# A fused adaLN / sliding-attention / token-MLP block on one core: modulation blocks on ScalarE's queue, x in two loads, other warming matmuls, another order

## The chip, the cores and the metric

The kernel runs on one core of one Trainium2 chip. A core has TensorE (PE in the profile; PEld are its weight loads), VectorE (DVE), ScalarE (ACT), GpSimd (POOL) and SyncE (SP), which issues DMAs. The metric is the device time of one execution in microseconds; 203.5 us is the median of three runs before the change (203.14 to 203.56).

## The reference

x is 2048 tokens by 512 channels. A conditioning vector c gives six modulation vectors; two of them act in the first layernorm, one scales the attention's output, two act in the second layernorm, and one scales the MLP's output. Attention has 32 heads of 16 channels, and each token looks at itself and at 7 earlier tokens, two apart. The MLP mixes over tokens (2048 to 1792 to 2048), not over channels.

```python
mod = (_silu(c) @ w_mod).reshape(c.shape[0], 6, 1, -1)      # sa, ca, ga, sb, cb, gb
h = _layernorm(x) * (1 + ca) + sa
x = x + ga * _A_ref(h, A_wqkv, A_wo)                        # local attention: W = 8, dilation 2
h = _layernorm(x) * (1 + cb) + sb
x = x + gb * _B_ref(h, B_w1, B_b1, B_w2, B_b2)              # layernorm, gelu(h.T @ w1 + b1) @ w2 + b2, transposed back
```

## The kernel before

The program is a list of named operations with their dependencies (`_Graph`). The text `ORDER` lists every name in the order of issue; `name:a` or `name:v` puts an operation that can run on two engines on ScalarE or VectorE, and a digit gives it one of four PSUM slots `ps0` to `ps3` of two banks each. `schedule()` checks that the order respects the dependencies, and each engine executes its own operations in that order. A DMA is an instruction of the queue that issues it: `dma(...)` takes SP's unless it is told `"act"`. So an engine whose next instruction waits holds back all that stand behind it, DMAs too. All operations are recorded through one helper, so nearly all profile rows have the line L179, and one goes by tiles.

The start. `ld_c` loads c, and `cps` (TensorE) turns it into a column, `silu_exp` (ScalarE) and `silu_dve` (VectorE) make silu of it. `ld_wmodA` and `ld_wmodB` bring two halves of the columns of `w_mod` that the first layernorm needs (512 KB each, rows of 2 KB) into the buffer `vD0`. `modcols0` and `modcols1` multiply them by silu(c) into columns, and `modcols_h` and `modcols_cp` bring these to SBUF as `sacol` and `a1col`. Meanwhile tokens 0 to 511 (chunk 0: four tiles of 128 tokens, loaded by `ld_x00`, `ld_x01`, `ld_x02`) get their layernorm: `ln1s` (statistics: two VectorE instructions, or four of ScalarE), `rstd1` (Ln and Exp on ScalarE, with one Ln for each run of neighbouring tiles whose statistics came from the same engine), `nb1`, `ln1n` (the normalised tile). `tr0_..` transposes them on TensorE, and `hT0_0` to `hT0_3` evict them to `hTb`, with scale `a1col` and shift `sacol`. `warm0` to `warm4` are matmuls of the identity with itself, whose result nobody reads.

Then four chunks of 512 tokens run, interleaved. For each: projections `qkvk`, `qkvq`, `qkvv` (TensorE) with evictions `evk`, `evq`, `evv`; `vd` copies that spread v over partitions by window position (16 DMAs a chunk on SP); `qk0` to `qk3` (VectorE products q times shifted k) with `red` (TensorE sums them per head); `max`, `sub`, `exp`, `sum`, `rb`, `smul` (the softmax); `a2` and its eviction `a2ev`; `pv0` to `pv3` (VectorE, weights times v) with `pvacc`; `oev`; `wo` (output projection plus residual); `x1ev`, `x1sq`, `rstd2`, `t`, `aff` (second layernorm), `ln3s`, `rstd3`, `h3` (the MLP's own layernorm). The MLP's first matmul is done in two halves over tokens: `mlp1_0_<fc><fl>_0` and `_4` take chunks 0 and 1, `park0` keeps that half in SBUF as bf16, and `mlp1_1_..` take chunks 2 and 3; `gadd`, `gelu` and `gbm` finish it. `mlp2` is the second matmul, `xb` prepares x plus bias, `fin` adds, `st_out` stores. `modrows` makes the other four modulation vectors from `ld_wmod2` to `ld_wmod5`; `biascols` brings the biases in as columns; `ld_w1_..` and `ld_w2_..` load the MLP's weights into buffers that became free.

Of the kernel before, what the change touches and what calls it, by code (L numbers as in the profile page):

```python
# [32 lines left out]
evk0_0:v ln1s8:a qkvq0_1:1 ln1n4:v ln1n5:v ld_wmod2 qkvv0_0:0 evq0_0:v evk0_1:a ln1n7:v evq0_1:a qk0_0 ln1s10:a  # L33
tr1_10:2 tr1_00:3 qkvq0_2:1 evv0_0:a hT1_0:v qk0_1 hT1_2:a qkvv0_2:0 hT1_1:a rstd1_2_0 evq0_2:a nb1_2_0 ln1n11:v
red0_0:3 ln1n9:v hT1_3:a red0_1 qk0_2 biascols:1 evv0_2:a qkvk1_0:2 ln1s12:a vd0_130 vd0_121 qkvq1_0:0 qk0_3 vd0_111
khalo1:a ln1s14:a vd0_030 vd0_010 red0_2 evk1_0:a biascols_cp ld_wo1 red0_3 ln1n8:v ln1n10:v vd0_100 qkvq1_2:1
evq1_0:a max0 vd0_031 ln1s15:a vd0_000 qk1_0 sub0 vd0_020 qkvk1_2:2 vd0_001 exp0 vd0_131 evq1_2:a qk1_1 vd0_011 sum0
vd0_120 tr2_10:0 rb0 red1_0:1 ld_wo3 evk1_2:a modrows:3 vd0_110 smul0 hT2_2:a vd0_021 qk1_2 a2_0:2 vd0_101 hT2_3:a
red1_1 mrow_ev tr2_00:0 a2ev0:a bc0 qkvv1_2:3 qk1_3 ln1s13:a qkvv1_0:2 hT2_0:a pv0_0 hT2_1:a red1_2 khalo2:a rstd1_3_0
red1_3 evv1_0:a qkvq2_0:0 nb1_3_0 max1 vhalo1:a evv1_2:a pv0_1 ln1n15:a pvacc0_0:2 vd1_031 sub1 ln1n12:a vd1_000  # L40
qkvk2_0:3 exp1 vd1_001 vd1_030 pv0_2 ln1n13:a vd1_130 sum1 evq2_0:a vd1_011 pvacc0_1 evk2_0:a vd1_100 qkvv2_2:0 pv0_3
vd1_010 oev0_1:a vd1_020 rb1 vd1_131 qkvk2_2:3 evv2_2:a vd1_021 gmul vd1_110 ln1n14:a pvacc0_2:2 vd1_120 smul1
evk2_2:a pvacc0_3 vd1_101 qk2_0 a2_1:1 oev0_3:a tr3_00:0 vd1_111 tr3_10:3 vd1_121 a2ev1:a wo2:2 bc2 qk2_1 hT3_2:a
ld_w1_0_3 wo3:1 bc1 hT3_3:a hT3_0:a wo1:3 x1ev3 pv1_0 x1ev2 wo0:1 hT3_1:a x1ev1 qkvq2_2:2 pv1_1 x1sq3 x1sq2 pvacc1_0:0
x1ev0 x1sq1 pv1_2 pvacc1_1 qkvv2_0:3 x1sq0 khalo3:a rstd2_0_0 vhalo2:a evq2_2:a nb2_0_0 pv1_3 warm2:1 t2:a red2_0:1
red2_1 evv2_0:a pvacc1_2:2 qk2_2 pvacc1_3 oev1_1:a vd2_010 qkvq3_0:3 vd2_100 oev1_3:a vd2_030 t1:a vd2_000 t3:v wo7:0
qk2_3 evq3_0:a vd2_120 vd2_110 wo6:2 t0:a vd2_111 x1ev7 wo5:3 vd2_021 aff0_0 x1ev6 vd2_020 x1sq7 wo4:0 ld_w1_0_1 x1sq6
vd2_031 red2_2 x1ev5 ld_w1_0_0 ln3s0_0:v red2_3 x1ev4 qkvk3_0:2 ln3s0_2:v ln3s0_3:v vhalo3:a x1sq5 x1sq4 qkvv3_0:3
ln3s0_1:v vd2_121 rstd2_1_0 evk3_0:a vd2_101 nb2_1_0 max2 t4:a qk3_0 sub2 t6:a qkvk3_2:0 rstd3_0_0 t7:a evv3_0:a
nb3_0_0 qkvv3_2:2 t5:v h3_2:v h3_0:v exp2 aff1_0 evk3_2:a sum2 qkvq3_2:3 evv3_2:a h3_1:v rb2 vd3_031 h3_3:v ln3s1_1:a  # L50
smul2 mlp1_0_10_0:0 vd3_020 ln3s1_0:v vd2_131 mlp1_0_30_0:2 ln3s1_3:a vd3_030 ln3s1_2:v mlp1_0_11_0 ld_w1_0_6 qk3_1
vd2_011 a2_2:1 evq3_2:a mlp1_0_31_0 vd2_001 rstd3_1_0 ld_w1_0_4 mlp1_0_00_0:3 a2ev2:a nb3_1_0 h3_5:v mlp1_0_01_0
h3_4:v h3_7:a pv2_0 red3_0:1 h3_6:a red3_1 mlp1_0_31_4 qk3_2 vd3_110 mlp1_0_10_4 vd2_130 mlp1_0_01_4 vd3_001
mlp1_0_11_4 vd3_130 qk3_3 vd3_000 mlp1_0_00_4 park0_1:a red3_2 park0_0:a pvacc2_0:0 pv2_1 red3_3 mlp1_0_60_0:3
mlp1_0_60_4 max3 vd3_121 pvacc2_1 mlp1_0_30_4 vd3_011 oev2_1:a pv2_2 vd3_101 sub3 vd3_010 mlp1_0_40_0:0 exp3 vd3_120
mlp1_0_41_0 park0_3:a vd3_021 pv2_3 sum3 vd3_111 mlp1_0_61_0 rb3 vd3_100 pvacc2_2:2 vd3_131 smul3 pvacc2_3 ld_w1_0_2
ld_w1_0_5 a2_3:1 oev2_3:a mlp1_0_61_4 a2ev3:v wo9:2 park0_6:a pv3_0 wo8:1 x1ev9 ld_w1_1_0 x1sq9 mlp1_0_41_4 pv3_1
x1ev8 wo11:3 ld_w1_1_3 pvacc3_0:2 x1ev11 wo10:1 pv3_2 x1sq11 ld_w1_1_1 x1sq8 pvacc3_1 mlp1_0_40_4 x1ev10 pv3_3 x1sq10
mlp1_0_20_0:3 oev3_1:a mlp1_0_21_0 rstd2_2_0 pvacc3_2:1 nb2_2_0 t11:v pvacc3_3 t10:a t9:v mlp1_0_21_4 t8:v oev3_3:a
aff2_0 mlp1_0_20_4 park0_4:a wo13:2 ld_w1_1_2 park0_2:a ld_w1_1_5 wo12:1 bc3 x1ev13 ln3s2_0:v x1sq13 ln3s2_2:v wo14:0  # L60
ld_w2_0 x1ev12 ln3s2_3:v wo15:3 x1sq12 ln3s2_1:v rstd2_3_0 mlp1_0_50_0:2 rstd3_2_0 nb2_3_0 t13:v mlp1_0_50_4 x1ev15
nb3_2_0 ld_w2_7 h3_9:v x1ev14 h3_8:v mlp1_0_51_0 h3_10:v x1sq15 t12:v h3_11:v mlp1_0_51_4 x1sq14 aff3_0 mlp1_1_00_0:1
rstd2_3_2 park0_5:a nb2_3_2 mlp1_1_30_0:3 t14:v t15:v ln3s3_0:a aff3_2 mlp1_1_31_0 ld_w2_2 mlp1_1_50_0:0 ln3s3_1:a
ln3s3_3:v mlp1_1_51_0 ln3s3_2:v mlp1_1_01_0 rstd3_3_0 rstd3_3_2 mlp1_1_10_0:2 nb3_3_0 h3_13:v ld_w1_1_4 h3_12:a
nb3_3_2 h3_14:v mlp1_1_11_0 h3_15:v xb2 mlp1_1_11_4 ld_w1_1_6 mlp1_1_10_4 mlp1_1_00_4 gadd1 ld_w2_3 mlp1_1_31_4 gelu2
mlp1_1_01_4 gelu3 mlp1_1_30_4 gadd0 mlp1_1_50_4 ld_w2_1 gadd3 gelu1 mlp1_1_51_4 gelu0 mlp1_1_20_0:2 gelu7 mlp1_1_21_0
gelu6 gbm7 gbm0 mlp1_1_21_4 gbm3 ld_w2_6 gadd5 mlp1_1_20_4 gbm1 gelu11 mlp1_1_40_0:1 gadd2 mlp1_1_41_0 gbm6 gelu5
mlp1_1_40_4 gbm2 ld_w2_4 gbm11 gelu10 gbm5 mlp1_1_41_4 gelu4 mlp1_1_60_0:3 gadd4 mlp1_1_61_0 gbm4 gelu8 mlp1_1_60_4
gbm10 gelu9 gbm8 mlp1_1_61_4 gbm9 xb1 mlp2_1_0_0:0 gadd6 xb3 gelu13 gelu12 mlp2_0_0_0:2 gbm12 gbm13 mlp2_5_0_0:1
mlp2_1_12_0 mlp2_3_0_0:3 fin1_0 xb0 st_out1_0 mlp2_3_12_0 mlp2_2_0_0:0 fin3_0 st_out3_0 ld_w2_5 mlp2_2_12_0 xb7  # L70
mlp2_6_0_0:3 fin2_0 xb5 st_out2_0 mlp2_6_12_0 mlp2_4_0_0:0 xb6 fin6_0 mlp2_0_12_0 mlp2_5_12_0 fin0_0 mlp2_8_0_0:3
fin5_0 st_out5_0 st_out6_0 st_out0_0 mlp2_7_0_0:2 xb4 mlp2_4_12_0 mlp2_10_0_0:1 fin4_0 st_out4_0 mlp2_8_12_0 xb8
mlp2_7_12_0 mlp2_11_0_0:0 fin7_0 fin8_0 st_out8_0 st_out7_0 mlp2_13_0_0:2 xb11 xb9 mlp2_11_12_0 xb10 mlp2_10_12_0
mlp2_9_0_0:3 fin10_0 fin11_0 st_out10_0 mlp2_9_12_0 xb14 mlp2_15_0_0:1 fin9_0 st_out9_0 mlp2_15_12_0 mlp2_13_12_0
st_out11_0 mlp2_12_0_0:0 xb15 xb12 mlp2_12_12_0 xb13 mlp2_14_0_0:3 fin13_0 fin12_0 st_out12_0 st_out13_0 mlp2_14_12_0
mlp2_15_0_256:2 fin14_0 fin15_0 st_out14_0 mlp2_15_12_256 st_out15_0 fin15_256 st_out15_256
"""


# [864 lines left out]
```

## Time and profile before

| what | value |
|---|---|
| median of three runs | 203.5 us (203.14 to 203.56) |
| the profiled execution's own time | 205.16 us |
| its span, first to last instruction | 203.5 us |
| mean granted TensorE clock | 0.992 |
| busy in the span | PE 194.1, DVE 157.6, ACT 126.3, POOL 4.3 us |
| eight warming matmuls of `warm0` | 1.42 to 5.01 |
| landing of the second modulation block | 9.86 |
| first ScalarE eviction of a transposed tile (`hT0_2`) | 12.18 |
| first projection matmul | 13.21 |
| end of `a2ev2` (ScalarE, attention weights of chunk 2) | 91.71 |
| end of the last product of chunk 3 (VectorE) | 98.44 |
| last normalised tile of the MLP (`h3_15`) | 134.55 |

Times inside the execution are microseconds from the start of the span. A busy time counts instructions that the engine executes; matmuls overlap one another, and the ends of TensorE's rows are modelled, so its real progress is read from starts: a matmul with 512 columns starts every 0.216 us at full clock and every 0.427 us at half. On VectorE and ScalarE an instruction of some size starts about 0.1 us before the one ahead of it has ended.

### The profile page before, as it was taken

The numbers are of one execution on the slowest core, as the hardware profiler recorded it, in microseconds if no ns is written. First come the engines' busy times: TensorE is split into PE (matmuls) and PEld (weight loads), VectorE is DVE, ScalarE is ACT, GpSimd is POOL, SyncE is SP. The second block draws the span as 40 slices with busy tenths as digits, with TensorE's granted clock in tenths as the row PEclk, the third lists the DMA queues.
The fourth block names the chain that finished last, engine by engine and source line by source line (L and its number), as shares of the span: only waits on it lengthen the run. The fifth ranks groups of instructions, "written<-read, shape, count | busy, mean of one in ns | idle before, by whom it ended". The sixth has DMA issues, their size and how long they took to land.

```text
span 203.5 us, 3374 instructions
## 1 busy us (share of the span) xinstructions
PE 194.1 (95%) x1276; PEld 91.4 (45%) x1296; DVE 157.6 (77%) x206; ACT 126.3 (62%) x261; POOL 4.3 (2%) x30
## 2 busy tenths in 40 slices
...
GB/s 132 332 358 269 297 90 164 161 101 109 177 162 137 93 153 252 33 212 221 68 180 204 293 95 314 290 290 293 290 212 0 29 138 94 77 26 55 71 56 53
DMA packets 42179, 33.48 MB, mean 165 GB/s; under 512 B 2100, under 2 KB 39604, under 8 KB 42164
## 3 DMA queue, kind: packets, MB, share of 16 engines
...
q14 instruction: 5, 0.04, 0.1%
q10 hardware_dynamic: 8, 0.00, 0.0%
...
## 4 chain that ended last, share of the span: by engine, by line
PE 56%; ACT 33%; DMA 3%; issue 3%; DVE 3%; SPq 1%; ACTq 0%; DVEq 0%
PE ps L179 56%; ACT junk L179 8%; ACT hTb L179 4%; DMA vD<-in_w_mod_dram 3%; ACT v_c L179 3%; ACT k_c L179 3%; ACT q_sb L179 3%; ACT h L179 2%; ACT xx L179 2%; ACT o_sb L179 2%; ACT lv L179 2%; DVE prod L179 1%; ACT n_sb L179 1%; DVE pvb L179 1%; ACT ee L179 1%
## 5 line engine op out<-in xcount | busy, mean ns | idle before, releaser
L179 DVE TENSOR_TENSOR prod<-q_sb,k_c 128x4096 bf16<-128x4096 bf16 x16 | 36.1, 2282 | 0.0
L179 DVE TENSOR_TENSOR pvb<-a2sb,vD 128x4096 bf16<-128x4096 bf16 x16 | 35.9, 2285 | 0.1
L179 PE MATMUL ps<-h,wst 128*128 128x512 bf16 x125 | 29.0, 380 | 0.3 <-issue 0.2
L179 PEld LDWEIGHTS <-wst 128*128 128x128 bf16 x128 | 12.2, 98 | 15.8 <-issue 1.6
L179 PE MATMUL ps<-gT,vD 128*128 128x512 bf16 x81 | 18.6, 379 | 0.2
L179 PE MATMUL ps<-woq,o_sb 128*128 128x512 bf16 x62 | 16.3, 379 | 0.1
L179 PE MATMUL ps<-hTb,w_k 128*128 128x512 bf16 x61 | 15.1, 385 | 0.6 <-ACT hTb L179 0.5
L179 DVE TENSOR_TENSOR k_c<-ps,k_c 128x512 bf16<-128x512 f32 (+1 forms) x9 | 5.5, 631 | 12.9 <-PE ps L179 10.8
L179 PE MATMUL ps<-hTb,w_q 128*128 128x512 bf16 x62 | 15.2, 381 | 0.1
L179 DVE TENSOR_TENSOR q_sb<-ps,q_sb 128x512 bf16<-128x512 f32 x8 | 5.4, 689 | 12.6 <-PE ps L179 12.5
L179 PEld LDWEIGHTS <-o_sb 128*128 128x128 bf16 x106 | 10.3, 98 | 10.2 <-issue 0.9
L179 PEld LDWEIGHTS <-w_q 128*128 128x128 bf16 x96 | 9.9, 109 | 10.9 <-issue 1.9
L179 PE MATMUL ps<-hTb,w_v 128*128 128x512 bf16 x62 | 14.7, 380 | 0.1
L179 PEld LDWEIGHTS <-vD 128*128 128x128 bf16 x116 | 9.1, 97 | 12.2 <-DMA vD<-in_w_mod_dram 2.3
L179 PEld LDWEIGHTS <-w_k 128*128 128x128 bf16 x80 | 8.9, 112 | 9.5 <-issue 1.7
L179 PE MATMUL ps<-gT,prod 128*128 128x512 bf16 x56 | 12.6, 379 | 0.0
L179 PE MATMUL ps<-gT,pvb 128*128 128x512 bf16 x55 | 12.5, 379 | 0.1
L179 PEld LDWEIGHTS <-w_v 128*128 128x128 bf16 x80 | 8.5, 111 | 8.6 <-issue 0.8
L179 ACT ACTIVATE junk<-xx,su 128x512 bf16<-128x512 bf16 x16 | 11.6, 725 | 0.4
L179 PEld LDWEIGHTS <-ident 128*128 128x128 bf16 (+1 forms) x79 | 7.1, 107 | 9.6 <-issue 4.5
L179 ACT ACTIVATE hTb<-ps,sacol,a1col 128x512 bf16<-128x512 bf16 x12 | 8.8, 784 | 3.4 <-PE ps L179 3.4
L179 ACT ACTIVATE o_sb<-ps 128x1024 bf16<-128x1024 f32 x8 | 8.0, 1019 | 4.4 <-PE ps L179 4.4
...
## 6 DMA issues: line engine op xcount, KB each, us to landing
...
```

Source lines behind the costliest of these rows:

```text
L179: r = fn(*a, **k)
```

## The change

- `ld_wmodA` and `ld_wmodB` are issued by ScalarE's queue. There the order is `ld_c`, `act_table`, `ld_wmodA`, `silu_exp`, `ld_wmodB`, `rstd1_0_0`.
- Chunk 0's x comes in two loads of two tiles each, `ld_x00` first; `ld_x01` is gone.
- The warming matmuls are nine groups (8, 6, 4, 4, 3, 3, 3, 2, 2) and no longer five (8, 4, 3, 3, 3): `warm0`; then `warm1`, `warm3` and `warm6` before the first transposes; `warm8` and `warm2` between the last transposes of chunk 0 and the first projection; `warm5` among the `wo` of chunk 1; `warm7` and `warm4` among the first `mlp1`.
- The order is new on every engine, and 28 operations change between ScalarE and VectorE, all of them statistics, norms or small evictions (`ln1s`, `ln1n`, `ln3s`, `t`, `h3`, `evk0_0`, `evq0_0`). On GpSimd `halo0` comes before `consts2`.

```diff
-consts ld_x02 ld_c consts2 warm0:0 ld_x01 act_table ld_x00 ld_wmodA ld_wmodB ld_b1 ln1s3:v ln1s2:a ld_b2 cps:1 ln1s0:v
-warm3:2 ld_x1 halo0 ld_w1a silu_exp ln1s1:v rstd1_0_2 ld_w1b warm1:3 ld_x2 nb1_0_2 silu_dve rstd1_0_0 ld_w0 ln1n2:a
-modcols0:0 nb1_0_0 ln1n0:v ld_w2 modcols1 ln1n1:v ln1n3:a sc_rep tr0_10:2 modcols_h tr0_00:3 modcols_cp tr0_02
-ld_wmod5 tr0_12 hT0_0:v warm4:1 hT0_2:a hT0_1:v ln1s7:a hT0_3:v ld_wo2 qkvk0_0:0 ln1s5:v ld_wo0 qkvk0_2:1 ld_wmod4
-ln1s6:v ln1s4:a ln1s9:v ld_wmod3 qkvk0_1:3 rstd1_1_0 ln1s11:v qkvk0_0b evk0_2:a qkvq0_0:2 nb1_1_0 ld_x3 ln1n6:v
...
+consts ld_x00 ld_c halo0 consts2 warm0:0 cps:1 ld_x02 act_table ld_wmodA silu_exp ld_wmodB ld_x1 ld_w1a ld_w1b ld_x2
+ld_w0 ln1s0:v ln1s1:v rstd1_0_0 ln1s3:a silu_dve sc_rep nb1_0_0 ln1s2:v ln1n1:v ln1n0:v rstd1_0_2 ld_w2 ld_x3 ld_wmod4
+ld_wo0 ld_b1 ld_wmod5 ld_b2 ld_wmod3 ld_wmod2 nb1_0_2 ln1n2:v ln1n3:v warm1:2 warm3:3 warm6:0 tr0_10:1 modcols0:2
+modcols1 tr0_00:3 tr0_02 tr0_12 modcols_h modcols_cp hT0_0:v hT0_1:v hT0_2:a hT0_3:v ln1s4:v ln1s5:v warm8:0 warm2:2
+qkvk0_0:0 qkvk0_0b qkvk0_2:3 qkvk0_1:2 ln1s6:a ln1s7:a evk0_2:a rstd1_1_0 evk0_0:a qkvq0_0:1 qkvq0_1:3 qkvv0_2:0
+ln1s9:v ln1s10:v ln1s11:v nb1_1_0 ln1s8:v evq0_0:a ln1n6:a ln1n7:a evk0_1:a evq0_1:a evv0_2:a rstd1_2_0 ln1n5:v
...
+oev1_3:a qkvq3_0:2 wo7:0 qk2_3 t3:v qk2_2 t1:a t2:a khalo3:a evq3_0:a x1ev7 aff0_0 wo6:3 red2_2 red2_3 wo4:2 warm5:0
+wo5:0 x1ev6 vhalo3:a x1sq6 x1sq7 x1ev4 ln3s0_3:a x1ev5 x1sq4 x1sq5 max2 ln3s0_0:v ln3s0_1:v ln3s0_2:v qk3_0 qkvk3_2:3
...
+ld_w1_0_4 vd3_020 vd3_001 ld_w1_0_6 vd2_101 mlp1_0_30_0:0 warm7:1 mlp1_0_10_0:2 a2_2:1 mlp1_0_11_0 warm4:3 mlp1_0_31_0
+red3_0:3 qk3_1 a2ev2:a nb3_1_0 red3_1 h3_6:v h3_5:v h3_4:a h3_7:a mlp1_0_00_0:1 mlp1_0_01_0 pv2_0 qk3_3 qk3_2
+mlp1_0_01_4 mlp1_0_00_4 mlp1_0_10_4 mlp1_0_31_4 mlp1_0_30_4 mlp1_0_11_4 park0_0:a park0_3:a park0_1:a pv2_1 red3_2
+red3_3 mlp1_0_60_0:1 pvacc2_0:0 max3 pvacc2_1 mlp1_0_61_0 sub3 pv2_2 oev2_1:a exp3 pv2_3 mlp1_0_60_4 mlp1_0_61_4 sum3
...
+ln3s2_3:v ln3s2_2:v ln3s2_1:v x1sq13 x1ev12 x1sq12 rstd2_3_0 rstd3_2_0 xb3 nb3_2_0 h3_9:v h3_11:v nb2_3_0 h3_8:v t12:v
...
+mlp2_7_12_0 mlp2_6_12_0 xb5 fin5_0 xb6 fin6_0 xb4 xb7 fin4_0 fin7_0 st_out4_0 st_out7_0 st_out6_0 st_out5_0 ld_w2_6
+ld_w2_7 mlp2_9_0_0:0 mlp2_11_0_0:1 mlp2_11_12_0 mlp2_8_0_0:2 mlp2_8_12_0 mlp2_10_0_0:3 mlp2_10_12_0 mlp2_9_12_0 xb8
...
@@ -240,7 +240,7 @@
-    WARM=(8, 4, 3, 3, 3),
+    WARM=(8, 6, 4, 4, 3, 3, 3, 2, 2),
...
@@ -387,11 +387,11 @@
     dma(c_t[:], c[0].rearrange("(t p) -> t p", p=P), 1024, [], ["c_t"], "ld_c", "act")
-    for i, n_ in ((0, 1), (1, 1), (2, 2)):
+    for i, n_ in ((0, 2), (2, 2)):
         dma(xx[:, i:i + n_, :], x_view[:, i:i + n_, :], n_ * P * D * 2, [], [("xx", i + k) for k in range(n_)],
             f"ld_x0{i}")
-    dma(wmodA[:, 0:2, :], wmod_view[:, 0:2, 0:2 * D], 2 * D * P * 2 * 2, [], vdk[0][4:], "ld_wmodA")
-    dma(wmodA[:, 2:4, :], wmod_view[:, 2:4, 0:2 * D], 2 * D * P * 2 * 2, [], vdk[0][:4], "ld_wmodB")
+    dma(wmodA[:, 0:2, :], wmod_view[:, 0:2, 0:2 * D], 2 * D * P * 2 * 2, [], vdk[0][4:], "ld_wmodA", "act")
+    dma(wmodA[:, 2:4, :], wmod_view[:, 2:4, 0:2 * D], 2 * D * P * 2 * 2, [], vdk[0][:4], "ld_wmodB", "act")
```

More of the change, by code (lines that the diff above doesn't have):

```diff
@@ L33 @@
[L33 to L76, printed above, removed]
+consts ld_x00 ld_c halo0 consts2 warm0:0 cps:1 ld_x02 act_table ld_wmodA silu_exp ld_wmodB ld_x1 ld_w1a ld_w1b ld_x2
@@ new lines @@
+ln1n4:v qk0_0 qk0_1 qkvq0_2:1 tr1_10:2 tr1_00:3 qkvv0_0:0 evq0_2:a hT1_2:a khalo1:a hT1_3:a hT1_0:v nb1_2_0 ln1s12:v
+ln1n11:v hT1_1:a evv0_0:a red0_0:1 red0_1 qkvk1_0:2 biascols:3 qkvq1_0:0 ln1s13:a ln1n10:a ln1n8:a evk1_0:a evq1_0:a
+ln1s14:a vd0_010 vd0_030 vd0_021 ld_wo3 vd0_101 vd0_000 vd0_020 vd0_111 vd0_001 vd0_011 ld_wo2 vd0_121 vd0_110 vd0_100
+vd0_120 vd0_031 qk0_2 qk0_3 biascols_cp ln1n9:v red0_2 red0_3 qkvq1_2:3 max0 sub0 qkvk1_2:2 evq1_2:a exp0 qk1_0 qk1_1
+sum0 tr2_10:0 red1_0:3 evk1_2:a rb0 modrows:2 smul0 hT2_2:a khalo2:a hT2_3:a mrow_ev vhalo1:a qk1_2 red1_1 tr2_00:1
@@ new lines @@
+a2_0:0 qk1_3 hT2_0:a a2ev0:a qkvv1_2:2 qkvv1_0:0 pv0_0 ln1s15:a hT2_1:a evv1_2:a rstd1_3_0 evv1_0:a qkvk2_2:1
+pvacc0_0:2 red1_2 red1_3 nb1_3_0 pv0_1 max1 qkvq2_0:0 pvacc0_1 sub1 ln1n13:a evk2_2:a ln1n12:a ln1n15:a ln1n14:a
+evq2_0:a exp1 qkvk2_0:1 tr3_00:0 sum1 vd0_130 ld_wo1 bc0 vd0_131 vd1_001 vd1_030 vd1_011 vd1_010 vd1_021 vd1_000
+vd1_020 vd1_120 vd1_121 vd1_031 vd1_131 vd1_110 vd1_100 vd1_130 bc1 vd1_111 vd1_101 oev0_1:a evk2_0:a rb1 hT3_0:a
+pv0_2 pv0_3 gmul smul1 qkvv2_2:2 pvacc0_2:1 pvacc0_3 a2_1:3 evv2_2:a oev0_3:a hT3_1:a vhalo2:a a2ev1:a qkvv2_0:2
@@ new lines @@
+mlp1_0_20_0:3 x1ev10 x1sq10 x1sq11 rstd2_2_0 oev3_1:a mlp1_0_21_0 mlp1_0_21_4 pvacc3_2:1 pv3_3 nb2_2_0 t8:a t10:v
+t11:v t9:v pvacc3_3 mlp1_0_20_4 oev3_3:a aff2_0 mlp1_0_40_4 park0_2:a wo13:0 park0_4:a wo12:1 x1ev13 ln3s2_0:v
+ln3s2_3:v ln3s2_2:v ln3s2_1:v x1sq13 x1ev12 x1sq12 rstd2_3_0 rstd3_2_0 xb3 nb3_2_0 h3_9:v h3_11:v nb2_3_0 h3_8:v t12:v
+t13:v h3_10:v wo15:3 wo14:2 mlp1_0_50_0:0 mlp1_0_51_0 mlp1_0_51_4 mlp1_0_50_4 x1ev14 x1ev15 x1sq15 x1sq14 aff3_0
+rstd2_3_2 nb2_3_2 park0_5:a ln3s3_0:a ln3s3_1:a mlp1_1_10_0:1 mlp1_1_11_0 mlp1_1_00_0:2 mlp1_1_01_0 mlp1_1_50_0:3
```

20 lines of the change are left out of this document (added).

## The prediction

> **What bounds the kernel now.** I read the chain that ended last first, whole and then in order of time. Its engine line says that TensorE is busy on only 56% of it and ScalarE carries 33%; columns of the pieces are start, length, what (all us).
>
> ```profile
> PE 56%; ACT 33%; DMA 3%; issue 3%; DVE 3%; SPq 1%; ACTq 0%; DVEq 0%
> ```
>
> ```profile
> 2.74 7.11 DMA vD<-in_w_mod_dram
> 9.86 0.05 issue
> 9.90 2.25 PE ps L179 x32
> 12.16 0.02 issue
> 12.18 0.78 ACT hTb L179
> ...
> 90.59 0.21 ACT rs L179
> 90.81 0.02 issue
> 90.83 0.17 DVE nb L179
> ...
> 96.15 2.29 DVE prod L179
> 98.45 0.04 issue
> 98.49 0.94 PE ps L179 x9
> ```
>
> So there are four stretches. Until 9.86 the second modulation block (`ld_wmodB`) travels, 7.11 us from its issue. Until 12.18 TensorE makes the modulation columns and the first transposes. From 12.18 to about 91 ScalarE is the chain, op after op. From 91 to 98.5 it is VectorE's products, and from 98.49 to the end TensorE without a break. The stretches by engine (length; busy us of PE, PEld, DVE, ACT):
>
> ```profile
> 12.20:91.70 79.50, 77.16 (x606) 37.50 (x615) 76.82 (x84) 78.24 (x164) 0.00 (x0) 0.99 0.79 168
> 98.50:134.80 36.30, 35.98 (x243) 15.58 (x247) 34.42 (x49) 29.29 (x67) 0.00 (x0) 1.00 0.92 214
> ```
>
> ScalarE does 78.24 of 79.50 us: full, with TensorE and VectorE barely behind. Nothing can be won there except by fewer ScalarE microseconds or an earlier start. The start, microsecond by microsecond (the last three columns are granted clock, DMA share, GB/s), and its waits:
>
> ```profile
> 8.00:9.00 1.00, 0.42 (x16) 0.42 (x16) 0.46 (x2) 0.76 (x2) 0.00 (x0) 1.00 1.01 352
> 9.00:10.00 1.00, 0.23 (x10) 0.15 (x7) 0.00 (x0) 0.00 (x0) 0.00 (x0) 1.00 1.02 352
> 11.00:12.00 1.00, 1.00 (x12) 1.00 (x11) 0.24 (x1) 0.00 (x0) 0.00 (x0) 0.50 1.09 362
> ACT hTb L179 <- PE ps L179: 3.4, 1, 3.4
> PE ps L179 <- DMA vD<-in_w_mod_dram: 1.7, 2, 0.9
> ```
>
> TensorE starves for the two blocks, and the granted clock falls to 0.50 from 10.4 to 13.8. The 16 first transposes therefore come every 0.107 us (10.32 to 12.14), where chunk 1's come every 0.056.
>
> **The change part by part**, against the profiled execution: 205.16 us of its own, span 203.5, so 1.7 around it. The median of the runs, 203.5, is 1.7 lower than 205.16; I carry the difference over to it.
>
> *Loads.* Block A leaves SP and is issued by ScalarE after the table load, which ends at 2.67: 2.70 instead of 2.27. Block B is now queued on ScalarE behind `silu_exp`, which waits for TensorE's `cps`, itself behind eight half-speed warming matmuls (4.94 to 5.12). `silu_exp` ran at 5.16 to 5.33, so B is issued at 5.4 instead of 2.74. ScalarE pays 0.45 (SP's rows) to 0.56 (its own `ld_c` row) for each issue; the one behind B, `rstd1_0_0`, waits until 5.9 and nothing needs it before the block lands. SP, rid of 0.43 + 0.47 and of one x issue (0.45), issues chunk 1's x at 1.8 instead of 4.17, and this now travels beside the blocks. When does B land? No row has two busy queues. Lower bound: the 256 KB x load took 2.8 from issue, plus 256 KB more at the 350 GB/s of the windows, 0.75: 5.4 + 3.5 = 8.9. Upper: B's own 7.11 of before: 12.5. I take 10.4, near the middle: first packet 1.1 after the issue, as the trace has it for the first x load, 512 KB at half of 340 GB/s 3.1, and 0.8 for the last packets and the completion (before, 15 of 16 packets had started by 8.3, the last ended at 9.47, and the landing is at 9.86).
>
> The Trainium skill, "DMA: Bandwidth & Descriptors", section on queues, rings and completion order, says that each DMA engine goes round its queues packet by packet; by equal packets the blocks' rows (2 KB against 1 KB of x) would have two thirds of the bandwidth, and the sum would be 0.8 better. It also says that ScalarE's and SP's rings lie on the same 16 engines, which speaks against any gain from a second queue; no run here shows either.
>
> *From B to the first hT.* Before: 12.18 - 9.86 = 2.32, of it 0.56 columns and 16 transposes. One group of four now stands before the columns, 12 follow. TensorE has 13 warming matmuls from 5.05 (0.427 each until the clock rises at 7.0, then 0.216: done at 8.8), a transpose group 0.23, A's columns 0.55: busy to 9.6 with one hole of under a microsecond. So I take the full clock: 0.04 + 0.56 + 12 x 0.056 + 0.1 = 1.4 (half clock: 2.0). The normalised tiles 2 and 3 are later (VectorE: stats 0.84 and four norms 0.41, behind ScalarE's 1.56 stat and `rstd1_0_2`: 9.9 against 8.76), still before B. ScalarE's first hT: 10.4 + 1.4 = 11.8, **-0.4**. The 2 + 4 warmers before the first projection take 1.3, where VectorE's first two hT (0.54 + 0.46) take 1.0: 0.3, hidden, since the first ScalarE eviction is queued behind two stats (3.1).
>
> *ScalarE's share, `hT0_2` to `a2ev2`.* Out: five stats (1.47 net of overlap) and three norms (0.70), 9.44. In: three stats, five norms, two small evictions (0.48), 8.87. The stats of a group now stand together by engine, so `rstd` needs three Ln pieces of 0.28 less: 0.84. By rows 78.63 becomes 77.22: **-1.4**. Before, it took 79.53 for 78.63. New idle follows: `evk1_2` waits for TensorE some 0.2, `oev0_3` 0.15, smaller ones elsewhere. I take **+0.6**, between 0 and 1.4 (all the gain idle). VectorE's rows to `pv2_0` go from 78.79 to 78.52: nothing.
>
> *TensorE.* Warmers behind the first projection: 3 before, 8 after, 5 x 0.216 = 1.08. They stand (`warm5`, `warm7`, `warm4`) before matmuls that wait for ScalarE's evictions, up to `a2ev2`, hence nothing, or 1.08 if that cover is gone. After `a2ev2`, `mlp1_0_00`/`01` (1.73) come later than before, red3_0/1 (1.0) earlier; around the last product, red3_2 and pvacc2_0 (0.5 each, 0.1 of switching) follow instead of `mlp1_0_30_4` (0.86). I take **+0.4** between 0.25 and 0.75.
>
> *Tail of layernorm 3.* `xb3` (0.74) moves ahead of VectorE's last norms. Before, the last norm ended at 134.55 and its matmul began at 134.83, VectorE having idled 0.41 for `rstd3_3_0`: **+0.1**, at most 0.5.
>
> *No cost:* `halo0` ahead of `consts2` (two memsets, 0.23; consts2 ends at 5.8, its first reader is at 25); b1/b2 later (`biascols` at 26); SP's new order: `ld_w1_0_6` waits for chunk 3's v, is issued near 91 and with the 8.1 of the w_q row lands at 99.3, where 60_0 begins near 100 (0 to 0.5 if late); `ld_w2_6`/`7` go behind eight output stores, issued at 177 to 180, 10 us ahead of use.
>
> Sum: -0.4 - 1.4 + 0.6 + 0.4 + 0.1 = **-0.7**, span 202.8, own time 204.5, median 202.8.
>
> **The rivals.**
> (a) Block B late. For: B's issue is 2.65 later and shares its engines. Every microsecond of landing moves ScalarE's whole stretch. The gain is gone at 11.1, the loss passes 0.4 at 11.5; at 11.9 the time is 203.5 - 0.7 + 1.5 = 204.3. Against: 9.6, should the blocks' 2 KB rows get twice the share of x's 1 KB rows.
> (b) Half clock at the start all the same: 12 transposes at 0.107, +0.6; 203.4. For: the first 3.4 us with TensorE busy from 1.42 did not lift the clock; it fell at 10.39 after TensorE had been busy on half of the 3.41 us before. Against: the new share of that stretch is over 75%.
> The Trainium skill, "TensorE: Matmul & The Clock Gate", part 1, has the gate close after an idle window of about 3.4 us, free-running. By that rule (b) could not happen; the trace's fall after a half-busy stretch disagrees, and I go by the trace.
> (c) TensorE becomes the bound in chunks 1 to 3: its waits for free PSUM slots eat ScalarE's 1.4, and the five extra warmers are paid: -0.4 - 1.4 + 1.4 + 1.1 + 0.4 + 0.1 = +1.2, 204.7. It decides from 0.7 of new waits on ScalarE together with uncovered warmers. For: 77.2 of 79.5 us are TensorE's already. Against: the warmers stand before waits.
> (d) VectorE, full to 133, holds the end with `xb3` and its last norms, so nothing arrives: 203.4.
>
> **How the numbers follow.** Forecast 0.42 (own range 201.9 to 203.0), (a) 0.18, (b) 0.08, (c) 0.22, (d) 0.10. About 0.2%, 0.4 us, is what a measurement can tell from no change. Faster is the forecast, 0.42; within it (b) and (d), 0.18; slower (a) and (c), 0.40. Low 201.9 is B at 9.5; high 204.9 holds most of (a), whose bound of 12.5 gives just that, and of (c).
>
> **What would show it.** In the profile after: block B landing (10.4), the granted clock from 10 to 14 (1.0), ScalarE's first hT (11.8, before 12.18), `a2ev2`'s end (some 90.9, before 91.71), the last chunk-3 product (some 97.7, before 98.44), and no idle TensorE from there. Wrong if B lands after 11, if ScalarE idles over 1.4 before `a2ev2`, or if TensorE shows waits for PSUM evictions where the warmers stand.

## The result and the profile after

The changed kernel takes 209.29 us (208.80 to 210.72), the kernel before, run beside it, 203.53 (203.14 to 203.81): a ratio of 1.0296, 95% interval 1.0243 to 1.0349. It is slower by some 5.8 us, where 0.7 faster was forecast and 204.9 was the end of the range. (Here and below a ratio leaves out executions more than 1.5% above the fastest of their kernel, so it can differ from the quotient of the medians.) The profiled execution of after has 209.21 us of its own (span 207.5), only 4.05 above the profiled execution of before, which at 205.16 was 1.6 above its median: TensorE's clock was halved there from 10.4 to 13.8, as not in every execution of that kernel.

First the same view as before, the share of the engines in the chain that ended last. ScalarE's share fell from 33% to 25%, but DMA's rose from 3% to 10%:

```profile
PE 59%; ACT 25%; DMA 10%; issue 2%; DVE 1%; SPq 1%; ACTq 0%
```

The pieces of that chain in order of time (start, length, what; us):

```profile
1.44 4.51 DMA vD<-in_w_mod_dram
5.95 0.02 issue
5.97 7.46 DMA vD<-in_w_mod_dram
13.42 0.05 issue
13.47 5.46 PE ps L179 x38
...
94.35 0.92 ACT a2sb L179
95.28 0.04 issue
95.32 5.12 PE ps L179 x23
...
185.23 9.57 DMA o_sb<-in_B_w_dram
194.80 0.05 issue
194.85 7.96 PE ps L179 x43
```

The first five lines are the result. Block A travels from 1.44 to 5.95. Only then is block B issued (5.97), and it lands at 13.42, where it landed at 9.86 before. The later lines answer to the end of `a2ev2` (95.27; before 91.71) and to the last stretch, where a new DMA stands in TensorE's way (`ld_w2_7`, which loads into `o_sb`'s memory).

ScalarE's timeline around the issue (start, length, instruction; in brackets its idle time and what ended it):

```profile
4.94 0.17 ACT L179 ACTIVATE ecol<-ps 128x4 f32<-128x4 f32 x1 [2.26 <-PE ps L179]
5.97 0.38 ACTq L179 DMA_DIRECT2D vD<-in_w_mod_dram  x1
```

`silu_exp` is over at 5.11, and block B's issue follows 0.86 later. What it waits for stands in the trace's records of the issues, which name semaphores (counters that a landing raises): block A's landing raises number 104, and block B's issue waits for 104 and raises it again. In this program the DMAs of both queues take eight semaphores in turn, and from the ninth on each waits until the one eight places ahead has landed. In that turn block A is the fifth and block B the thirteenth, so B waits for A, whose landing the chain shows at 5.95. Nothing in the data asks for it.

The start by the microsecond (busy time of PE, PEld, DVE, ACT, POOL; granted clock, DMA share, GB/s), and the two stretches that were shown of before:

```profile
9.00:10.00 1.00, 0.45 (x18) 0.35 (x15) 0.89 (x3) 0.04 (x1) 0.00 (x0) 1.00 1.11 350
10.00:11.00 1.00, 0.00 (x0) 0.00 (x0) 0.01 (x1) 0.00 (x0) 0.00 (x0) 1.00 1.08 360
12.00:13.00 1.00, 0.00 (x0) 0.00 (x0) 0.00 (x0) 0.00 (x0) 0.00 (x0) 0.50 1.09 366
16.00:17.00 1.00, 1.00 (x4) 0.44 (x3) 0.79 (x2) 0.97 (x4) 0.00 (x0) 0.50 1.11 349
```

```profile
15.39:95.27 79.88, 78.05 (x622) 37.95 (x631) 76.13 (x84) 77.09 (x157) 0.00 (x0) 0.98 0.75 152
101.99:138.65 36.66, 36.34 (x257) 15.56 (x260) 34.57 (x50) 29.80 (x68) 0.00 (x0) 1.00 1.03 244
```

From 10 to 13.4 no compute engine has work, while the DMA engines move 350 to 370 GB/s. They are full, but block B's first packet starts only at 10.14. What was carried before and after that shows in the packets, bytes (MB) and busy shares of the two queues (q1 is SP's, q10 ScalarE's), first from 6 to 10.13, then from 10.5 to 12:

```profile
q1 hardware_dynamic: 1521, 1.49, 108.8%
...
q10 hardware_dynamic: 176, 0.36, 67.5%
q1 hardware_dynamic: 184, 0.19, 37.5%
```

For 4 us the engines carry SP's loads alone; once block B has started, its packets (2 KB) and SP's (1 KB) go about one for one, and it has two thirds of the bytes. And in the hole the granted clock falls to 0.50, from 11.3 until 18.1, well after TensorE's work has begun again at 13.47. TensorE's timeline shows both:

```profile
13.47 0.59 PE L179 MATMUL ps<-sc,vD 128*128 128x1 bf16 x16 [4.02 <-DMA vD<-in_w_mod_dram]
13.92 1.44 PE L179 MATMUL ps<-ident,n_sb 128*128 128x128 bf16 x12
15.15 2.77 PE L179 MATMUL ps<-ident 128*128 128x512 bf16 x6
17.71 1.65 PE L179 MATMUL ps<-hTb,w_k 128*128 128x512 bf16 x5
```

TensorE is idle for 4.02 us; then come 12 transposes 0.107 apart and six warming matmuls 0.427 apart, both at half speed, before the first projection (17.71; before 13.21).

Where the 4.05 us of the two profiled executions lie:

| stretch | before | after | difference |
|---|---|---|---|
| to ScalarE's first hT (`hT0_2`) | 12.18 | 15.39 | +3.21 |
| to the end of `a2ev2` | 79.53 | 79.88 | +0.35 |
| to the end of chunk 3's last product | 6.73 | 6.72 | 0 |
| to the `wo` matmul that waited for it (`wo9`) | 9.61 | 9.89 | +0.28 |
| to the last normalised tile | 26.50 | 26.54 | +0.04 |
| to the end of `fin15_256` | 66.34 | 66.60 | +0.26 |

The start holds four fifths of it. The stretch that should have become 0.8 shorter did not, and this too comes from the start, as the experiments show.

### The profile page after: what moved, and what is told of

Its sections match the earlier page's. It is cut to its first block, busy times and chain, and to the rows that moved or that the text cites. A ratio compares the mean times of both kernels' runs of the same rounds, so it can differ in the third digit from the quotient of the medians.

```text
span 207.5 us, 3398 instructions
## 1 busy us (share of the span) xinstructions
PE 195.5 (94%) x1288; PEld 92.2 (44%) x1310; DVE 157.0 (76%) x208; ACT 123.8 (60%) x252; POOL 4.3 (2%) x30
## 4 chain that ended last, share of the span: by engine, by line
PE 59%; ACT 25%; DMA 10%; issue 2%; DVE 1%; SPq 1%; ACTq 0%
PE ps L179 59%; DMA vD<-in_w_mod_dram 6%; ACT junk L179 6%; DMA o_sb<-in_B_w_dram 5%; ACT v_c L179 3%; ACT xx L179 2%; ACT k_c L179 2%; ACT hTb L179 2%; ACT o_sb L179 2%; ACT q_sb L179 2%; ACT h L179 1%; ACT a2sb L179 1%; ACT n_sb L179 1%; ACT lv L179 1%; ACT ee L179 1%
## 5 line engine op out<-in xcount | busy, mean ns | idle before, releaser
L179 PEld LDWEIGHTS <-w_q 128*128 128x128 bf16 x96 | 9.9, 109 | 10.5 <-issue 1.5
L179 PEld LDWEIGHTS <-ident 128*128 128x128 bf16 (+1 forms) x93 | 8.4, 105 | 10.4 <-issue 3.2
L179 PE MATMUL ps<-ident 128*128 128x512 bf16 x35 | 11.3, 474 | 1.4 <-POOL epscol L179 1.4
```

Source lines behind the costliest of these rows:

```text
L179: r = fn(*a, **k)
```

## The experiments

The theory that this profile suggests: block B is late, and what makes it late is the bytes that SP has issued ahead of it, since both queues are served in the order of issue. The rivals: ScalarE's queue as such is slow while SP's has work; the new order of the engines costs time by itself; the extra warming matmuls do; or the half clock is the greater part. "MB ahead" below is all that had been moved when block B's first packet started, counted in the packet records. As the engines move at a nearly constant rate, it says little more than when that was; the table at the end therefore sets beside it the bytes that were outstanding at block B's issue.

### Block B issued right behind block A

```diff
-act_table ld_wmodA silu_exp ld_wmodB ld_x1
+act_table ld_wmodA ld_wmodB silu_exp ld_x1
```

> The changed kernel with one thing undone: ScalarE issues block B right behind block A, ahead of silu_exp. In the changed kernel B was issued at 5.97 and its first packet moved at 10.1, its last at 12.8, landing 13.42. Theory F (the DMA engines serve what was issued first, whichever queue issued it: B stood behind some 3.5 MB of x and projection weights that SP had issued before 5.97): B, issued near 2, lands between 7 and 9, the start is then set by the normalised tiles 2 and 3 (10.0), hT0_2 begins at 11.3 to 12.3 instead of 15.4, and the median is 205.0 to 206.5 (209.3 before). Rival Q (ScalarE's queue gets only what SP's leaves as long as SP has packets; A was quick because SP's stream had only begun): B's packets still wait until SP's stream thins out at 10, landing 11 to 13, median 207.5 to 209.3.

Measured: 203.08 us (202.36 to 205.96) against 204.56 (203.11 to 205.83) of the kernel before; ratio 0.994 [0.9905, 0.9976]. One word moved in the order takes back the whole loss and a little more. TensorE's timeline, to be set against that of after:

```profile
8.60 0.94 PE L179 MATMUL ps<-sc,vD 128*128 128x1 bf16 x32
9.40 0.83 PE L179 MATMUL ps<-ident,n_sb 128*128 128x128 bf16 x12
10.07 1.46 PE L179 MATMUL ps<-ident 128*128 128x512 bf16 x6
11.36 1.89 PE L179 MATMUL ps<-hTb,w_k 128*128 128x512 bf16 x8
```

All 32 column matmuls run in one piece, so both blocks have landed by 9.0; the transposes come 0.056 apart, the first projection at 11.36 and not at 17.71, with the clock full from 6.1 on. Block B was issued at 1.88, its first packet started at 5.38 with 1.16 MB ahead. It was on ScalarE's queue as in after, while SP's stream ran: the queue as such is not slow. It came out better than expected because the new order, freed of the late start, gains: from `hT0_2` to the end of `a2ev2`

```profile
10.27:88.69 78.42, 77.35 (x632) 37.70 (x631) 76.34 (x84) 77.05 (x157) 0.00 (x0) 1.00 0.83 178
```

78.42 us, where before needs 79.53, with half clock at its start, and 79.52 at full clock (below).

### Both blocks on SP's queue, the new order kept

```diff
-    ... vdk[0][4:], "ld_wmodA", "act")
-    ... vdk[0][:4], "ld_wmodB", "act")
+    ... vdk[0][4:], "ld_wmodA")
+    ... vdk[0][:4], "ld_wmodB")
```

> The changed kernel with both blocks back on SP, behind the two x loads of chunk 0 and ahead of chunk 1's x. F and Q alike: B lands between 8.5 and 10, hT0_2 at 11.3 to 12.3, median 205.0 to 206.5. What is left above 203.5 is then the price of the new order itself with its warming matmuls; if the order's ScalarE rows (1.4 us fewer) were worth what was forecast, the median is below 203.5.

Measured: 203.31 us (202.46 to 205.24), ratio 0.9944 [0.9908, 0.998]. Block B is issued at 2.32 with 1.10 MB ahead and is taken up at 9.40; the ScalarE stretch is 78.60. With an early issue either queue gives the same time.

### The kernel before, with the blocks moved to ScalarE's queue alone

```diff
-    ... vdk[0][4:], "ld_wmodA")
-    ... vdk[0][:4], "ld_wmodB")
+    ... vdk[0][4:], "ld_wmodA", "act")
+    ... vdk[0][:4], "ld_wmodB", "act")
```

> The kernel before with the queue change alone: both blocks on ScalarE's queue, one behind the other, ahead of ScalarE's first statistics; order and warming matmuls as before. F: both are issued by 3, ahead of chunk 1's x, and land by 9.9 at the latest, so 202.5 to 203.8, no worse than before. Q: B lands between 10.5 and 13, 204.3 to 207.

Measured: 204.61 us (203.77 to 206.62), ratio 1.0014 [0.9977, 1.0051]: no difference that can be measured. In the order of before block B's issue follows A's at once (1.42 and 2.22), and its first packet starts 3.22 after its issue, much as on SP (3.48 and 3.18 in the two profiles of before). The chain shows what was late in its place:

```profile
1.80 5.84 DMA xx<-in_A_x_dram
...
12.78 0.78 ACT hTb L179
```

SP's load of one x tile (128 KB), issued at 1.80 behind block A's 512 KB on the other queue, landed only at 7.64, 5.84 after its issue; in before, with block A behind it, it took 3.27 (1.79 to 5.06). From 4.0 to 4.5 SP's queue started one packet of 1 KB, ScalarE's 78 of 2 KB. So a load can be held up by bytes that the other queue issued ahead of it, here in the other direction.

### The kernel before, unchanged

> The kernel before, unchanged, for a second profile: its profiled execution (205.16, span 203.5) lies 1.7 above the median of its runs, while the changed kernel's profiled execution (209.21) lies on its median. If the profiled one was an unlucky position of the clock's windows (half clock from 10.4 to 13.8), another profile shows a span near 201.8 with the granted clock at 1.0 or 0.5 elsewhere in the first 14 us; if profiles are 1.7 slower as such, the span is 203.5 again.

Measured: 204.72 us (202.84 to 205.75), ratio 1.0000 [0.9959, 1.0041]. Its profiled execution was the one at 202.84, and its chain reads

```profile
2.75 5.56 DMA vD<-in_w_mod_dram
...
8.36 1.48 PE ps L179 x32
...
9.87 0.78 ACT hTb L179
```

The same program: block B needed 5.56 from its issue, not 7.11, the clock stayed at 1.0, and `hT0_2` began at 9.87, not at 12.18. From there to the end of `a2ev2` it takes as long as the first profile, which ran at half clock until 13.8:

```profile
9.87:89.39 79.52, 77.31 (x616) 37.20 (x615) 77.03 (x84) 78.27 (x164) 0.00 (x0) 1.00 0.82 177
```

So the shorter stretch of 78.42 above comes from the new order and not from the clock. In this comparison the unchanged kernel has 41 executions: in 13 the mean granted clock was 0.999 or 1.000, and they took 202.84 to 204.25 us; in the others it was 0.983 to 0.992 (a stretch of 3.4 us at half makes 0.992), and they took 203.96 to 205.83. Of the ten with block B behind A, eight had 0.999 or 1.000. Between the executions at full clock alone the medians are 203.67 and 202.95: of the 1.5 us by which that version is faster, about half is that its start is more often free of the half clock, and 0.7 the rest.

### The path to `silu_exp` shortened

`silu_exp` waits for `cps`, which stands behind `warm0`. Five of its eight matmuls go to `warm1`:

```diff
-    WARM=(8, 6, 4, 4, 3, 3, 3, 2, 2),
+    WARM=(3, 11, 4, 4, 3, 3, 3, 2, 2),
```

> The changed kernel with the first warming group cut from 8 to 3 matmuls and the next raised from 6 to 11, so that cps, silu_exp and with them block B's issue come about 2 us earlier (near 3.5 instead of 5.97); B still stands behind silu_exp on ScalarE. Theory F (service in the order of issue over both queues): fewer bytes are ahead of B (two to two and a half MB instead of 3.7), its first packet moves between 6.5 and 8.2 instead of 10.1, it lands between 9 and 11, and the median is 204 to 206.5. Rival Q (ScalarE's queue waits until SP's stream thins out): first packet at 10 again, landing 13, median 208.5 to 209.5.

Measured: 208.40 us (205.93 to 209.64) against 204.69 (203.99 to 206.03), ratio 1.0113 [1.0076, 1.0151] (the quotient of the medians is 1.018). The profiled execution is the one at 205.93, with the clock full. The chain:

```profile
1.31 3.64 DMA xx<-in_A_x_dram
4.95 0.02 issue
4.97 7.34 DMA vD<-in_w_mod_dram
```

The five other executions had mean clocks of 0.984 to 0.992 and took 207.57 to 209.64. This was a miss: the first packet came at 8.90, with 2.44 MB ahead, and the landing (12.31) and the median lie above what was expected. Here it was no longer `silu_exp` that held block B's issue: it stood now eleventh in the turn of the semaphores and waited for the third DMA, an x load, until 4.95, so that it came at 4.97 and not near 3.5. From the issue to the first packet it took 3.93, hardly less than in after, and one microsecond earlier at the issue gave 1.1 at the landing. This also limits the theory: SP had finished issuing the same loads by 4.97 here as by 5.97 in after (3.1 MB in all), and yet block B's first packet started after 2.44 MB here and after 2.87 there. Strict service in the order of issue would have made it start behind the same bytes; it passed some of them.

### The hole filled with warming matmuls

`warm6` moves between the two groups of column matmuls and gets 19 matmuls, `warm3` 7; block B stays late.

```diff
-... warm1:2 warm3:3 warm6:0 tr0_10:1 modcols0:2
-modcols1 ...
+... warm1:2 warm3:3 tr0_10:1 modcols0:2 warm6:0
+modcols1 ...
-    WARM=(8, 6, 4, 4, 3, 3, 3, 2, 2),
+    WARM=(8, 6, 4, 7, 3, 3, 19, 2, 2),
```

> The changed kernel with the 4 us hole of TensorE ahead of modcols1 filled by 19 warming matmuls behind modcols0 (and warm3 with 7, so that as many as before stand ahead of the transposes). B still lands near 13.4. If the half clock (11.3 to 18.1 in the changed kernel's profile) costs what its rows say, it stays at 1.0, the 12 transposes take 0.7 instead of 1.3, the six warmers and first projections half of what they took, and the median falls by 1.2 to 2.2, to 207.1 to 208.1. If ScalarE's queue hides all but the transposes, it falls by 0.6 at most: 208.7 or more.

Measured: 207.92 us (207.26 to 209.22) against 204.69, ratio 1.0159 [1.0123, 1.0195]. TensorE's timeline:

```profile
9.32 4.26 PE L179 MATMUL ps<-ident 128*128 128x512 bf16 x19
13.42 0.54 PE L179 MATMUL ps<-sc,vD 128*128 128x1 bf16 x16
...
14.49 1.46 PE L179 MATMUL ps<-ident 128*128 128x512 bf16 x6
15.79 1.46 PE L179 MATMUL ps<-hTb,w_k 128*128 128x512 bf16 x5
```

Block B's columns start at 13.42, as late as in after (13.47), but the clock stays at 1.0: the transposes and the six warming matmuls go at full speed, the first projection is 1.92 earlier (15.79 against 17.71), and the profiled execution takes 207.26 against 209.21. So the half clock is worth 1.95 us of after between the two profiled executions, and 1.4% by the two ratios. The ScalarE stretch is 78.47 here too: after's 79.88 was the half clock's, which still slowed the first projections until 18.1. What remains against block B behind A, 4.9 us by the profiled executions and 2.2% by the ratios, is in the main the late landing itself (columns at 13.42 against 9.00).

### The warming matmuls in the middle taken out

Block B behind A, and `warm4`, `warm5` and `warm7` empty.

```diff
-    WARM=(8, 6, 4, 4, 3, 3, 3, 2, 2),
+    WARM=(8, 6, 4, 4, 0, 0, 3, 0, 2),
```

> The kernel with B issued right behind A (a_b_behind_a), with the three warming groups in the middle left out (warm4, warm5, warm7: 8 matmuls). If they stand in waits, as the prediction took it, the ratio to the kernel before stays at 0.994, within 0.002. If they are paid, 1.1 us go: 0.989.

Measured: 202.84 us (202.58 to 205.21), ratio 0.9919 [0.989, 0.9947], not to be told from 0.994 [0.9905, 0.9976] with them. The profiled stretches say it more sharply: 78.46 with none of the eight matmuls against 78.42, and 109.45 against 109.44 from `a2ev2` to the end. No run shows a price for them, as forecast.

### The two late weight loads ahead of the output stores

Block B behind A, and `ld_w2_6` and `ld_w2_7` moved right behind `ld_w2_1`.

```diff
-... ld_w2_0 ld_w2_1 h3_13:a ...
+... ld_w2_0 ld_w2_1 ld_w2_6 ld_w2_7 h3_13:a ...
-... st_out5_0 ld_w2_6
-ld_w2_7 mlp2_9_0_0:0 ...
+... st_out5_0
+mlp2_9_0_0:0 ...
```

> The kernel with B issued right behind A, with the last two loads of w2 ahead of the output stores instead of behind eight of them. In the changed kernel's profile the last of them was issued at 185.2 by SP's queue, landed at 194.8, and TensorE waited for it 0.1 to 0.6. If that wait is paid at the end the ratio falls by 0.001 to 0.002, to 0.992 to 0.993; if the load lands in time in this kernel, nothing changes.

Measured: 202.51 us (202.28 to 203.07) against 204.69, ratio 0.9884 [0.9861, 0.9908], the fastest of all versions and faster than both kernels. Its profile doesn't say by what: from `a2ev2` to the end it takes 109.44, just as without the move. Without the move TensorE does not wait for these weights either (the load, issued at 178.63, took 8.0 us; in after 9.57). In after the wait was in the list of waits (engine that waited, for whom, us in total, times, longest):

```profile
PEld L179 <- DMA o_sb<-in_B_w_dram: 0.6, 1, 0.6
```

The step from 0.994 to 0.9884 is therefore not shown to come from the edit; the granted clock was 0.998 to 1.000 in all five of its executions, which accounts for a part (at full clock, block B behind A has a median of 202.95).

### The bytes ahead of block B taken away, its late place kept

This separates the bytes ahead from being issued late. SP's loads behind chunk 0's x are held back by a copy of 1 KB within SBUF that needs silu(c); block B stays behind `silu_exp` on ScalarE's queue.

```diff
-... ld_wmodB ld_x1 ld_w1a ld_w1b ld_x2
-ld_w0 ln1s0:v ln1s1:v rstd1_0_0 ln1s3:a silu_dve sc_rep ...
+... ld_wmodB
+ln1s0:v ln1s1:v rstd1_0_0 ln1s3:a silu_dve hold ld_w1a ld_w1b ld_x1 ld_x2 ld_w0 sc_rep ...
+    dma(schold[:], sc[:], 1024, ["sc"], ["schold"], "hold")
```

> The changed kernel, with block B still issued by ScalarE behind silu_exp (at 5.97), but SP's next loads (the first weights, then chunk 1's x and the rest) stand behind a 1 KB copy of silu(c) within SBUF, which can be issued only once VectorE has made silu(c), at 5.95. So at B's issue only chunk 0's x and block A, 1.0 MB, have been issued ahead of it, where the changed kernel had about 2.7 MB. If a block waits for the bytes issued before it on either queue: first packet 1.1 to 1.7 us behind the issue, 7.0 to 7.7, landing 9.0 to 10.0, though it is issued as late as before. If it is ScalarE's queue, or a block's being issued late, that costs the 4.2 us from issue to first packet: first packet at 10.1 again, landing 12.5 or later. The time of the whole kernel is not the point, as the first weights and chunk 1's x are late too: 203 to 207.

Measured: block B was issued at 4.89, its first packet started at 5.92, 1.03 us later, with 1.10 MB ahead. The windows and TensorE's timeline:

```profile
5.00:6.00 1.00, 1.00 (x6) 0.48 (x5) 0.86 (x6) 0.58 (x4) 0.67 (x8) 1.00 0.14 52
6.00:7.00 1.00, 1.00 (x7) 0.44 (x5) 0.96 (x5) 0.97 (x3) 0.00 (x0) 1.00 0.40 102
7.00:8.00 1.00, 1.00 (x12) 0.48 (x11) 0.61 (x2) 0.97 (x5) 0.00 (x0) 1.00 0.94 334
8.00:9.00 1.00, 0.60 (x24) 0.52 (x22) 0.89 (x3) 0.04 (x1) 0.00 (x0) 1.00 0.39 104
```

```profile
8.84 0.55 PE L179 MATMUL ps<-sc,vD 128*128 128x1 bf16 x16 [0.40 <-DMA vD<-in_w_mod_dram]
```

Little moves from 5 to 6; block B then has the DMA engines nearly to itself and is taken up at 8.84, 3.95 after its issue, where after needs 7.50. It is taken up 4.6 us earlier than in after: 1.1 of them is the issue itself (with fewer DMAs ahead there is no semaphore to wait for, so it follows `silu_exp` at once), 3.5 the loads that SP no longer has on the way. The closest comparison is the run with `silu_exp` earlier: there block B was issued at 4.97, on the same queue and behind `silu_exp` too, with SP's loads on the way, and was taken up at 12.36. So it is neither the queue nor the late issue as such, but a late issue behind SP's loads. Where on the way from the issue to the DMA engines the block is held back, no run shows. The whole, one execution, takes 204.75 us, since the weights and chunk 1's x are now late: the first `evk` starts at 16.37, behind statistics on ScalarE that wait for chunk 1's x until 13.27.

### The kernel before, with block B behind `silu_exp` alone

```diff
-... ld_x00 ld_wmodA ld_wmodB ld_b1 ...
-... halo0 ld_w1a silu_exp ln1s1:v ...
+... ld_x00 ld_wmodA ld_b1 ...
+... halo0 ld_w1a silu_exp ld_wmodB ln1s1:v ...
-    ... vdk[0][:4], "ld_wmodB")
+    ... vdk[0][:4], "ld_wmodB", "act")
```

> The kernel before, with one part of the change alone: block B is issued by ScalarE right behind silu_exp (5.33 in the trace of before), block A and all else stay. By then SP has issued chunk 0's x, block A, chunk 1's x and the first weights, 2.0 to 2.3 MB. If a block waits for the bytes issued before it: first packet at 9.1 to 9.8, landing 12.2 to 13.1, ScalarE's first eviction at 14 to 15.5, and a time 2.5 to 4 us above the unchanged kernel's (ratio 1.012 to 1.020). If the late block costs only its own way (landing 5.4 plus 3.5 to 5 us, 9 to 10.4): ratio 0.998 to 1.004, and the loss of the changed kernel would be the work of its new order.

Measured: 210.11 us (209.82 to 210.36) against 204.25 (203.22 to 205.27), ratio 1.0289 [1.027, 1.0307]. This part of the change alone makes a loss as large as that of the whole change (1.0296). The equality is partly chance: block B's issue is 0.96 later still than in after, and the gain of the new order is missing. It is above the expected 1.012 to 1.020, and the chain says why:

```profile
2.74 4.17 DMA b_t<-in_B_b_dram
6.91 0.02 issue
6.93 7.61 DMA vD<-in_w_mod_dram
...
14.60 2.33 PE ps L179 x32
```

The issue did not come at 5.33 but at 6.93: by the turn of the semaphores block B (now the fourteenth) waited for the sixth DMA, a bias load of under 4 KB that had itself taken 4.17 behind the bytes ahead of it. With 2.67 MB ahead of the block it landed at 14.55, and the granted clock was 0.5 from 11.2 to 18.0.

### The way of block B in one table

| kernel | issue | MB outstanding at the issue | MB ahead | first packet after the issue | taken up |
|---|---|---|---|---|---|
| loads held back | 4.89 | 0.03 | 1.10 | 1.03 | 8.84 |
| before, unchanged, second profile | 2.75 | 0.79 | 1.11 | 3.18 | 8.36 |
| before, first profile | 2.74 | 0.83 | 1.11 | 3.48 | 9.90 |
| before, blocks on ScalarE's queue | 2.22 | 0.80 | 1.07 | 3.22 | 10.37 |
| new order, blocks on SP's queue | 2.32 | 0.96 | 1.10 | 4.02 | 9.40 |
| B behind A | 1.88 | 1.00 | 1.16 | 3.51 | 9.00 |
| before, B behind `silu_exp` | 6.93 | 1.80 | 2.67 | 3.89 | 14.60 |
| `silu_exp` earlier | 4.97 | 2.11 | 2.44 | 3.93 | 12.36 |
| after | 5.97 | 1.79 | 2.87 | 4.17 | 13.47 |

Outstanding are the bytes of all DMAs whose issue was over, on both queues, less those that had been moved. With next to nothing outstanding the first packet starts after 1.03 us. With 0.8 to 1.0 MB it starts 2.2 to 3.0 later, about the 2.3 to 2.9 that so many bytes take at the 0.35 MB in a microsecond of the windows. With twice as much it starts hardly later still (3.89 to 4.17): the block then passes part of what was issued ahead of it. So the wait is that of the outstanding loads (in the last three rows SP's), up to some 1.3 to 1.5 MB of them (what was moved between issue and first packet there); it is not strictly the order of issue, and no run shows what sets this limit.

This also says where after's lateness comes from. Against the first profile of before, block B is issued 3.23 later, its first packet waits 0.69 longer, and the rest of the way is 0.35 shorter: the late issue passes nearly whole to the landing, because the wait of some 4 us behind SP's loads stays.

## Why the prediction was wrong, step by step

**Block B's landing: the step that failed.** 10.4 was taken, between 8.9 and 12.5; it was 13.42. Three terms make the 3.0: the issue (5.4 forecast, 5.97 measured, +0.57, the wait for block A's landing by the turn of the semaphores, which the prediction did not look for), the first packet (1.1 after the issue forecast, 4.17 measured, +3.07), and the rest of the way (3.9 forecast, 3.28 measured, -0.62). The second is the failure. The 1.1 was the row of the first x load, which had nothing ahead of it, and with the loads held back it came true (1.03). The same paragraph had SP issuing chunk 1's x at 1.8, and did not go on to count what SP issues after it up to 5.4: weights and two more loads. It treated them as sharing the bandwidth with block B from its issue, not as standing before it. The profile of before had the better row: block B's own first packet there started 3.48 after its issue, on SP's queue behind 0.83 MB. The upper bound was B's own 7.11 of before; after's 7.46 is near it, and with the right issue it would have been 13.1. Block A, forecast to be issued at 2.70, was issued at 1.44: ScalarE's queue issued it while the table load still ran (1.41 to 2.69). This cost nothing.

The prediction cited the Trainium skill, "DMA: Bandwidth & Descriptors", section on queues, rings and completion order, by which each DMA engine goes round its queues packet by packet. From 10.5 to 12 after agrees: 176 packets of block B to 184 of SP's, and two thirds of the bytes. The cited rule says nothing of the wait that broke the forecast: from its issue at 5.97 to 10.14 not one packet of block B started, while SP's queue moved some 350 GB/s. So the prediction's third term, bandwidth shared from the first packet on, was sound (3.1 forecast, 2.70 from the first packet to the end of the last); what failed is that the sharing was taken to begin 1.1 after the issue. The other thing it took from that page, that a second queue is no second set of engines, agrees with the run that moved the blocks alone (1.0014).

**Rival (a), block B late,** was the mechanism, with 0.18 and 204.3; its bound at 12.5 was too low, and so the range ended at 204.9. Its price, a microsecond for a microsecond, was right once the clock is set apart: the forecast's own time of 204.5, plus the 3.0 of the landing, gives 207.5, and the run with the hole filled, late landing at full clock, took 207.26.

**The clock at the start** was taken as full; it was half from 11.3 to 18.1. TensorE's "one hole of under a microsecond" became two, of 0.85 and, since B was late, of 4.02: the greater follows from the first step. Rival (b) was also priced too low, at +0.6 for the 12 transposes. The six warming matmuls ahead of the first projection, "0.3, hidden", took 2.77 and not 1.46, and the first projections followed at half speed: 1.95 by the run with the hole filled. Against (b) stood a share of "over 75%" of busy TensorE in the stretch before the fall. These are the 3.41 us before it, in before and in after, and two stretches from the run with `silu_exp` earlier, whose profiled execution kept full clock though block B was late there too (the second number is TensorE's busy time):

```profile
6.98:10.39 3.41, 1.73 (x37) 1.06 (x36) 1.34 (x6) 1.75 (x4) 0.00 (x0) 1.00 0.99 335
7.85:11.26 3.41, 0.78 (x20) 0.69 (x20) 1.66 (x6) 1.16 (x5) 0.00 (x0) 1.00 1.09 356
...
7.65:11.06 3.41, 2.26 (x28) 1.34 (x26) 0.96 (x4) 0.46 (x3) 0.00 (x0) 1.00 1.08 362
11.06:14.48 3.42, 2.12 (x33) 1.58 (x34) 1.39 (x6) 0.83 (x2) 0.00 (x0) 1.00 1.10 351
```

TensorE was busy on 51% in before and 23% in after: the 13 warming matmuls were over by 7.8, not 8.8, as the clock had risen at 4.4 already, and block B was not there. On the gate, the Trainium skill ("TensorE: Matmul & The Clock Gate", part 1) has it close after an idle window of about 3.4 us on a free-running grid. The grid fits after: the clock rose at 4.43, fell at 11.26 and rose at 18.09, 6.83 apart each time, twice 3.41. The idle window does not: the clock fell 1.8 us into the hole, after a stretch in which TensorE had been busy on 23%, and in before on 51%. In the run with `silu_exp` earlier the clock had risen at 7.65, so the hole was split between two stretches of the grid, of 66% and 62%, and it stayed up. In all the profiles here, once the clock was up, it fell after stretches of the grid that were busy on 51% or less and stayed after those of 61% or more (estimates, as the ends of matmuls are modelled). Where the grid lies differs from execution to execution, so whether a late block also costs the half clock is in part luck.

**ScalarE's stretch**, -1.4 and +0.6: right in mechanism and size, though not in after. At full clock it was 78.42 to 78.60 in the versions of the new order, 0.9 to 1.1 under before's 79.53 (with the loads held back 80.55, as ScalarE waited for chunk 1's x), where -0.8 was forecast; ScalarE's busy time of 77.09 was forecast at 77.22. In after the half clock took it back (79.88).

**TensorE behind `a2ev2`,** +0.4 between 0.25 and 0.75: from its end to that of `fin15_256` 109.18 before, 109.44 in the versions without late landing, +0.26. After has another 0.3 (109.75).

**Warming matmuls in the middle at no cost, `xb3` at +0.1:** right (no difference without them; +0.04 up to the last normalised tile). So rivals (c) and (d) fell.

**`ld_w2_7`, "10 us ahead of use":** a small miss. It was issued at 185.23, 9.0 before TensorE wanted it, and took 9.57: 0.6 of waiting in after, and none with block B behind A.

**The start value.** The -0.4 at the start set the new order against one execution of before with half clock and block B at 9.86. The unchanged kernel also runs with neither (`hT0_2` at 9.87), so a gain of 2 us at the start was within the spread of the kernel before, and its first stretch should have been bounded by that. For the same reason the carried difference between 205.16 and the median of 203.5 failed. The 205.16 was an execution with half clock; the four runs of before beside after (203.14 to 203.81) lie where the unchanged kernel had full clock (202.84 to 204.25). In after half clock is in the profiled execution and in the median alike, and the two agree (209.21 and 209.29). So the median is 6.5 above the forecast of 202.8 by three terms: 3.0 of late landing, 1.95 of half clock, and 1.7 of this carried difference; the remaining -0.2 is the sum of all else.
